# Where layer 2's weights are split into two pieces, and in what order layer 2's own values are

## The chip, the cores and the metric

The kernel runs on one core of a Trainium2 chip, in one launch. The metric is the device time of one execution in microseconds (us); three runs of the kernel before gave 880.49, 882.21 and 882.72, with a median of 882.21. The core's engines are TensorE (PE; its weight loads are PEld), VectorE (DVE), ScalarE (ACT), GpSimd (POOL) and SyncE (SP), whose queue issues the transfers here.

## The reference

```python
attn = softmax(q, -1) @ (softmax(k, 2).T @ v)        # 4 batches, 8 heads, 576 tokens, 64 wide
x = attn as 2304 tokens x 512
x = silu(x @ w_in)  @ w_out                          # 512 -> 2048 -> 512, layer 1
y = mish(x @ w_in2) @ w_out2                         # the same sizes, layer 2; mish(h) = h * tanh(log(1 + e^h))
```

The weights arrive as 64-bit numbers; the kernel puts each together as a 32-bit one.

## The kernel before

**Two pieces.** TensorE multiplies float32 in a rounded form (fp32r). To keep precision each operand is split into a high piece (a cast by ACT) and a low piece (the value minus the high piece, by DVE or POOL), and a product is three matmuls: high by high, high by low, low by high.

**Layer 1** goes over the hidden units in two passes of eight chunks of 128. The second pass takes the tokens in five blocks (`WIDE`: 512, 512, 256, 512, 512). For each block and chunk c there is a first product G1 (x by w_in, 12 matmuls, then Silu on ACT, cast on ACT, subtraction on DVE) and, three chunks later (`SKEW`), a second product G2 (12 matmuls into four banks that collect the output). At the start of a token block the first four G1 stand one after the other. The list `events` holds these blocks; a block is one unit of its plan's time. x lies in the tile `xa`; the split copy `xs` of a token block is made five events before the block begins, and after that this block's part of `xa` is not read again.

**Layer 2's weights** are loaded and put together in that second pass, by a plan with due times (`w_plan`, `plan`): four weight tiles of 128 x 512 (two of w_in2, two of w_out2) for each of eight pairs of chunks. `w_take` asks for the load two takes ahead (three buffers `st`) and does the first step on ACT and DVE, `w_join` the second on DVE. `w_mix` and `o_mix` form sums of them on DVE, since layer 2 forms its products by Strassen and Winograd's scheme with seven products in place of eight. In the kernel before the unsplit sums go to HBM (`q_store`, into `wqf` and `wof`).

**Layer 2** takes the tokens in three strips (s) of 768, and in each the eight pairs of chunks, so 24 pairs, k = 0 to 23. A pair is seven steps. A step is a product (`prod`, six matmuls of 384 columns into bank 6 or 7) and, from k = 2 on, a `half` (nine matmuls of 256 columns) of the second product for the two pairs before. In pairs 0 and 1 three blocks left over from layer 1 stand in three of these places (`l1_rest`). From step 1, 3 and 5 ACT copies bank 6 (`keep`, tile sc); from step 2, 5 and 7 DVE adds bank 7 and the copy (tile hf) and ACT forms Mish; step 6 is Mish alone. `cut` splits a result into a tile g. `sum_g` forms four sums of the last pair's results on POOL, at step 1, and these are split at steps 1 to 4 (`old`). DVE's `gather` adds finished halves to the output in `xb`.

At the change to the next strip seven sums of x are formed (`x2_early` at pairs 6 and 14, `x2_late` at 7 and 15, on POOL) and split into the tiles x (`x2_part`): cast on ACT, and of two parts the first subtracted on DVE, the second on POOL.

In the first strip (k below 8) the weights come back unsplit from `wqf` and `wof` into the buffer `wall`; `q_split` and `o_split` split them there between the other work, on ACT and DVE and on ACT and POOL, and store both pieces in `wq` and `wo`. The halves trail by two pairs, so `o_split` goes on to pair 9. In the other strips the split weights are loaded as they are (1792 KB for w_in2 of one pair, 512 KB for a unit of w_out2; seven units for two pairs).

Every engine carries out its instructions in the order in which the program issues them (class `InOrder`), so an instruction that waits holds up all behind it. In layer 2 this order is that of the lines in `pair`, `fill` and `flush_lows`.

Of the kernel before, what the change touches and what calls it, by code (L numbers as in the profile page):

```python
# [65 lines left out]
def attention_silu_mish(ctx: ExitStack, tc: tile.TileContext, q, k, v, w_in1, w_out1, w_in2, w_out2, out):  # L66
# [25 lines left out]
    Q_PAIR, Q_RING, O_RING, O_NEAR = 3584, 3, 5, 3  # L92
# [33 lines left out]
    wo = [dp.tile([P, 1024], F32, name=f"wo{i}") for i in range(N_UNIT)]  # L126
    wqf = [dp.tile([P, Q_PAIR // 2], F32, name=f"wqf{i}") for i in range(NQ)]
    wof = [dp.tile([P, 512], F32, name=f"wof{i}") for i in range(N_UNIT)]
# [120 lines left out]
    def w_plan(start):  # L249
# [26 lines left out]
        for q in range(NQ):  # L276
            n = 2 * N0 + 4 * q
            a, b, *cs = boxes = [{} for _ in range(4)]
            for i, box in enumerate(boxes):
                plan((when(k + ev * i), w_take, n + i, box), (when(k + ev * i) + 1.0, w_join, box))  # L280
            mix = {}
            h = when(k + ev) + 1.2
            plan((when(k) + 1.4, q_store, a, "t", wqf[q][:, :512]), (h, w_mix, a, b, mix))
            plan((h + 0.4, q_store, b, "t", wqf[q][:, 512:1024]), (h + 0.4, q_store, mix, "t", wqf[q][:, 1024:1536]))
            plan((h + 0.4, q_store, mix, "z", wqf[q][:, 1536:]))
            c0, c1 = cs
            mo = {}
            h = when(k + 3 * ev) + 1.2
            plan((h, o_mix, c0, c1, mo))
            for box, what, half, i in (  # L290
                (c0, "t", 0, 0), (c0, "t", 1, 4), (c1, "t", 0, 1), (c1, "t", 1, 5), (mo, "t", 0, 3), (mo, "t", 1, 2), (mo, "z", 0, 6)
            ):
                plan((h + 0.4, q_store, box, what, wof[q // 2 * 7 + i][:, q % 2 * HD:(q % 2 + 1) * HD], half * HD))
            k += 4 * ev
# [26 lines left out]
    def w_mix(a, b, mix):  # L321

        a, b = (t["t"].bitcast(F32).rearrange("p (l n) -> p l n", l=2) for t in (a, b))
        u, z = (pools["tm"].tile([P, 512], U32, tag="wt", name="wt") for _ in range(2))
        mix["t"], mix["z"] = u, z
        u, z = (t.bitcast(F32).rearrange("p (l n) -> p l n", l=2) for t in (u, z))
# [447 lines left out]
    sums, lows = {}, []  # L774
# [34 lines left out]
    def x2_part(s, m):  # L809
        for k in range(2):  # L810
            t = sums[(s, m, k)]
            S.copy(x2[m][:, k, 0], t)
            lows.append((V if k == 0 else G, x2[m][:, k], t))

    def flush_lows():
        for e, to, t in lows:
            e.tensor_tensor(out=to[:, 1], in0=t, in1=to[:, 0].bitcast(F32), op=ALU.subtract)
        lows.clear()


    def q_unit(k, u):
        at, n = k % Q_RING * Q_PAIR + u * 1024, 256 if u == 3 else 512
        return wall[:, at:at + 2 * n].rearrange("p (i n) -> p i n", i=2)
# [12 lines left out]

    def q_split(k, *units):
        if k < NQ:
            for u in units:
                split(q_unit(k, u), V)  # L840
            if 3 in units:
                SP.dma_start(wq[k], wall[:, k % Q_RING * Q_PAIR:(k % Q_RING + 1) * Q_PAIR].bitcast(F32))
# [348 lines left out]
```

## Time and profile before

| | |
|---|---|
| median of three runs | 882.21 us |
| the profiled execution | 886.13 us, of which its span 884.3 |
| busy: PE, PEld, DVE, ACT, POOL | 841.9, 784.9, 556.1, 439.6, 233.5 us |
| DMA | 170.80 MB, mean 193 GB/s |
| mean granted TensorE clock | 0.985 |

All times in the profile are those of one execution, in us from its first instruction. Layer 1's second pass runs from about 285 to 472 us, layer 2 from there to the end. A row of the timeline gives a start, a length and an instruction; in brackets stand the time that the engine idled before it, and what ended the wait. Since nearly all calls go through one helper, most instructions carry the same line, L59, and are told apart by tiles.

### The profile page before, as it was taken

What the parts mean: (1) busy time and instruction counts of PE and PEld (TensorE: products, weight loads), DVE (VectorE), ACT (ScalarE), POOL (GpSimd) and SP (SyncE); (2) the same over time, 40 slices, a digit from 0 to 9 for tenths busy, and PEclk for the clock granted to TensorE, in tenths of its full rate; (3) what the DMA queues carried; (4) which work ended last, traced back from release to release, by engine and by line L of the source; (5) the groups of instructions that cost most, each with busy time, mean ns of one, the idle gap of its engine ahead of it and who ended that gap; (6) DMA issues with size and microseconds to landing.
All of it is one profiled execution on the core that took longest, in us unless ns stands there. A gap on an engine that the chain in (4) does not pass through costs nothing.

```text
span 884.3 us, 14216 instructions
## 1 busy us (share of the span) xinstructions
PE 841.9 (95%) x5314; PEld 784.9 (89%) x5314; DVE 556.1 (63%) x1043; ACT 439.6 (50%) x870; POOL 233.5 (26%) x239
## 2 busy tenths in 40 slices
PE   7799999999999999999999897978899998999997
PEld 6688988899999888898888887977899998999997
DVE  5898466673276566756753675658566658555555
ACT  5887254563245444444356555646444436444441
POOL 3035111221000000000031554469623438131310
PEclk9899999999999999999999999999899999999999
DMA  9986311310034359847626688889797666686634
GB/s 242 246 207 135 91 36 36 72 37 1 1 119 128 110 174 300 262 160 248 214 90 214 248 303 314 295 291 325 270 329 269 231 245 233 241 302 221 209 135 144
DMA packets 101028, 170.80 MB, mean 193 GB/s; under 512 B 34400, under 2 KB 73312, under 8 KB 97888
## 3 DMA queue, kind: packets, MB, share of 16 engines
q1 hardware_dynamic: 100960, 169.90, 58.6%
q8 instruction: 42, 0.69, 0.3%
q14 instruction: 26, 0.21, 0.1%
HBM read 121.11 MB, written 48.76 MB: 192 GB/s over the span
## 4 chain that ended last, share of the span: by engine, by line
PE 75%; DVE 6%; DMA 6%; ACT 5%; POOL 3%; issue 3%; SPq 2%; POOLq 0%; DVEq 0%; ACTq 0%
PE psum L59 57%; PE psum L57 18%; DMA wall<-wof 3%; DVE g L59 1%; DVE xb L59 1%; SPq L57 1%; POOL x L59 1%; DVE hf L59 1%; DMA xa<-in_k_dram 1%; DMA st<-in_moe_w_in_dram 1%; ACT g L59 1%; ACT xa L57 1%; ACT hf L59 1%; ACT wall L59 1%; POOL hf L59 1%
## 5 line engine op out<-in xcount | busy, mean ns | idle before, releaser
L59 PE MATMUL psum<-x,wall 128*128 128x384 f32 x1008 | 212.6, 348 | 24.8 <-DVE hf L59 17.1
L59 PE MATMUL psum<-wall,g 128*128 128x256 f32 x1512 | 207.2, 284 | 2.5 <-DVE xb L59 2.5
L59 PEld LDWEIGHTS psum<-wall,g 128*128 128x128 f32 x1512 | 202.0, 192 | 3.0 <-DVE xb L59 3.0
L59 PEld LDWEIGHTS psum<-x,wall 128*128 128x128 f32 x1008 | 176.1, 193 | 30.1 <-DVE hf L59 20.2
L59 DVE TENSOR_TENSOR g<-hf,g 128x384 fp32r<-128x384 f32 x168 | 109.7, 671 | 62.5 <-ACT g L59 61.9
L59 POOL TENSOR_TENSOR hf<-hf 128x384 f32<-128x384 f32 x92 | 98.2, 1068 | 143.8 <-ACT hf L59 138.4
L59 PE MATMUL psum<-g,wall 128*128 128x512 f32 (+2 forms) x624 | 129.7, 361 | 0.0
L59 PEld LDWEIGHTS psum<-g,wall 128*128 128x128 f32 x624 | 109.6, 189 | 14.9
L59 PE MATMUL psum<-xs,wall 128*128 128x512 f32 (+2 forms) x588 | 122.4, 362 | 0.0
L59 PEld LDWEIGHTS psum<-xs,wall 128*128 128x128 f32 x588 | 102.7, 188 | 14.9
L59 DVE TENSOR_TENSOR xb<-psum,xb 128x768 f32<-128x768 f32 (+2 forms) x94 | 80.1, 867 | 38.5 <-PE psum L59 38.4
L57 PE MATMUL psum<-xs,wall 128*128 128x384 f32 x468 | 100.4, 355 | 2.8 <-ACT gf L57 1.8
L59 ACT ACTIVATE hf<-hf 128x384 f32<-128x384 f32 x72 | 37.9, 526 | 112.6 <-DVE hf L59 112.6
L59 ACT CAST g<-hf 128x384 fp32r<-128x384 f32 x168 | 82.3, 513 | 21.5 <-POOL hf L59 16.6
L57 PEld LDWEIGHTS psum<-xs,wall 128*128 128x128 f32 x468 | 82.7, 193 | 7.0 <-ACT gf L57 3.2
L57 PE MATMUL psum<-g,wall 128*128 128x384 f32 x432 | 84.8, 343 | 0.0
L59 POOL TENSOR_TENSOR x<-xb,x 128x384 fp32r<-128x384 f32 x16 | 19.6, 1242 | 240.0 <-ACT x L59 240.0
L57 PEld LDWEIGHTS psum<-g,wall 128*128 128x128 f32 x432 | 74.7, 188 | 1.0 <-DVE g L57 0.2
L59 ACT ACTIVATE gf<-psum 128x512 f32<-128x512 f32 (+2 forms) x49 | 26.6, 543 | 95.8 <-PE psum L59 94.8
L59 DVE TENSOR_TENSOR g<-gf,g 128x512 fp32r<-128x512 f32 (+2 forms) x49 | 30.5, 624 | 66.5 <-ACT g L59 66.0
L59 ACT COPY sc<-psum 128x384 f32<-128x384 f32 x72 | 34.3, 477 | 56.8 <-PE psum L59 56.3
L59 POOL TENSOR_TENSOR wall<-wall 128x512 fp32r<-128x512 f32 x28 | 38.4, 1370 | 70.7 <-ACT wall L59 64.3
(133 smaller groups left out, 875.7 us busy)
## 6 DMA issues: line engine op xcount, KB each, us to landing
wall<-wq SPq DMA_DIRECT2D x16, 1792.0 KB, 8.7
wall<-wo SPq DMA_DIRECT2D x56, 512.0 KB, 4.2
st<-in_moe_w_in_dram SPq DMA_DIRECT2D x32, 512.0 KB, 5.0
st<-in_moe_w_out_dram SPq DMA_DIRECT2D x32, 512.0 KB, 4.5
wq<-wall SPq DMA_DIRECT2D x8, 1792.0 KB, 6.8
wo<-wall SPq DMA_DIRECT2D x28, 512.0 KB, 4.4
wof<-wt SPq DMA_DIRECT2D x56, 128.0 KB, 4.2
wall<-wof SPq DMA_DIRECT2D x28, 256.0 KB, 6.1
```

The costliest lines, as they stand in the source:

```text
L57: return call(*args, **kwargs)
L59: self.last = call(*args, **kwargs)
```

## The change

Layer 2's weights are split in layer 1's second pass, before they go to HBM. `t_high` casts a tile on ACT into one of eight strips of 512 columns in `xa` (the first 1024 tokens of x, which the second pass has read by then), `t_low` subtracts on POOL in place, `z_high` and `z_low` do the same for the narrow sums, and `put` stores both pieces into `wq` and `wo`, which are now the only copies. `wqf`, `wof`, `q_split`, `o_split` and their stores in layer 2 go; the first strip loads `wq` and `wo` as the others do. The pool of weight tiles (`tm`) has ten buffers in place of eight.

In layer 2, `cut` and `x2_part` no longer issue their casts and subtractions at once: they put them into the lists `casts` and `lows` with a due time in steps. `background`, once in each step, issues those that are due, and more while the time it counts for ACT and DVE (`COST` each, of `LONG` in a step) has room; `settle` issues what the next product or half needs. `sum_g` moves from step 1 to step 2, and all four sums enter the list there. At the strip changes POOL keeps three subtractions (`X_POOL`) of seven; before layer 2 DVE does all of them. At the end four sums on DVE are followed by their splits through the same list.

```diff
--- before.py
+++ after.py
...
@@ w_plan
-                plan((when(k + ev * i), w_take, n + i, box), (when(k + ev * i) + 1.0, w_join, box))
-            plan((when(k) + 1.4, q_store, a, "t", wqf[q][:, :512]), (h, w_mix, a, b, mix))
...
+                plan((when(k + ev * i), w_take, n + i, box), (when(k + ev * i + 1.0), w_join, box))
+            for i, mix in ((0, w_mix), (2, o_mix)):
+                a, b = boxes[i:i + 2]
+                m, z = {}, {}
+                h = k + ev * (i + 1) + 1.3
+                plan((when(h), mix, a, b, m, z))
+                for j, box in enumerate((a, b, m)):
+                    plan((when(h + 0.7 + 0.2 * j), t_high, box), (when(h + 1.1 + 0.2 * j), t_low, box))
+                plan((when(h + 1.3), z_high, z), (when(h + 1.7), z_low, z))
+                h += 1.9
+                if mix is w_mix:
+                    for j, box in enumerate((a, b, m)):
+                        to = wq[q][:, j * 1024:(j + 1) * 1024]
+                        plan((when(h), put, box, "hi", to[:, :512]), (when(h), put, box, "t", to[:, 512:]))
+                    plan((when(h), put, z, "t", wq[q][:, 3072:]))
...
+    def t_high(box):
+        i = strips["at"] = (strips["at"] + 1) % 8
+        box["hi"] = xaT[:, i % KC, i // KC * 512:(i // KC + 1) * 512]
+        S.copy(box["hi"].bitcast(F32R), box["t"].bitcast(F32))
+    def t_low(box):
+        G.tensor_tensor(out=box["t"].bitcast(F32R), in0=box["t"].bitcast(F32), in1=box["hi"], op=ALU.subtract)
...
+    def put(box, what, to):
+        t = box[what].bitcast(F32)
+        SP.dma_start(to, t if len(to.shape) == 2 else t.rearrange("p (i n) -> p i n", i=2))
...
@@ x2_part
-            S.copy(x2[m][:, k, 0], t)
-            lows.append((V if k == 0 else G, x2[m][:, k], t))
+            t, to = sums[(s, m, k)], x2[m][:, k]
+            if now is None:
+                S.copy(to[:, 0], t)
+                V.tensor_tensor(out=to[:, 1], in0=t, in1=to[:, 0].bitcast(F32), op=ALU.subtract)
+            else:
+                later_cut(to, t, now, due, (m, s), G if k and m in X_POOL else V)
+    X_POOL = (T2, T1, B22)
+    def later_cut(home, t, ready, due, tag, e=None):
+        serial[0] += 1
+        casts.append((due - 1, serial[0], ready, home, t, tag, V if e is None else e))
...
+    def settle(tag, now):
+        for z in [z for z in casts if z[5] == tag]:
+            one_cast(z, now)
+        for z in [z for z in lows if z[5] == tag]:
+            one_low(z)
+    def background(now, a_room, v_room):
+        while casts:
+            z = min((z for z in casts if z[2] <= now), default=None)
+            if z is None or (z[0] > now and a_room < COST):
+                break
+            a_room -= COST
+            one_cast(z, now)
+        while lows:
+            z = min((z for z in lows if z[2] <= now or z[0] <= now), default=None)
+            if z is None or (z[0] > now and v_room < COST):
+                break
+            v_room -= COST if z[6] is V else 0.0
+            one_low(z)
...
     def q_load(k):
-        if k < NQ:
-            for u in range(4):
-                w = q_unit(k, u)[:, 1].bitcast(F32)
-                SP.dma_start(w, wqf[k][:, u * 512:u * 512 + w.shape[1]])
-        elif k < NS * NQ:
+        if k < NS * NQ:
             SP.dma_start(wall[:, k % Q_RING * Q_PAIR:(k % Q_RING + 1) * Q_PAIR].bitcast(F32), wq[k % NQ])
-    def split(w, e):
-        S.copy(w[:, 0], w[:, 1].bitcast(F32))
-        e.tensor_tensor(out=w[:, 1], in0=w[:, 1].bitcast(F32), in1=w[:, 0].bitcast(F32), op=ALU.subtract)
...
-            split(o_slot(m).rearrange("p (i n) -> p i n", i=2), G)
-            SP.dma_start(wo[m], o_slot(m).bitcast(F32))
...
+    COST, SUM_AT = 0.58, 2
+    LONG, SHORT, REST = 2.13, 1.05, 3.77
-    def cut(k, name, t):
+    def cut(k, name, t, ready):
         home = slots.pop(0)
         gp[(k, name)] = home
-        S.copy(home[:, 0, :BLK], t)
-        lows.append((V, home, t))
+        use = (k // 2 * 2 + 2) * 7 + 1 + 2 * [z[0] for z in PHASES].index(name) + k % 2
...
+        later_cut(home, t, ready, use - 1, (k, name))
...
@@ pair
+        for i, (a, m, ps, start) in enumerate(ORDER, 1):
+            now = 7 * k + i
+            settle((m, s), now)
+            prod(k, a, m, ps, start)
+            a_room = v_room = LONG if k > 1 else REST if (k, i) in L1_AT else SHORT
...
+            if i == SUM_AT and k:
+                sum_g(k - 1, G, now)
...
+            background(now, a_room, v_room)
+            if i == 1 and q == NQ - 2 and s + 1 < NS:
+                x2_early(s + 1)
+            if i == 7:
+                q_load(k + Q_RING)
+            if pend:
+                half(*pend.pop(0))
...
-            for nm, nb in (("g", SKEW + 1), ("xs", 1), ("gf", 2), ("st", 3), ("tm", W_WAIT)):
+            for nm, nb in (("g", SKEW + 1), ("xs", 1), ("gf", 2), ("st", 3), ("tm", W_WAIT + 2)):
```

Three places in the engines' orders. On ACT, at the change to the last token block of layer 1 (gf is Silu's result, wt a weight tile, xs the split x of the block), before:

```order
L59 ACTIVATE gf<-psum 128x512
L59 CAST g<-gf 128x512
L59 CAST xs<-xa 128x512 x4
L59 ACTIVATE wt<-st 128x512 x3
L59 ACTIVATE gf<-psum 128x512
```

and there now:

```order
L59 ACTIVATE gf<-psum 128x512
L59 CAST g<-gf 128x512
L59 CAST xa<-wt 128x512 x3
L59 CAST xs<-xa 128x512 x4
L59 CAST wt<-wt 128x256
L59 ACTIVATE wt<-st 128x512 x2
L59 CAST xa<-wt 128x512 x3
L59 CAST wt<-wt 128x256
L59 ACTIVATE wt<-st 128x512
L59 CAST xa<-wt 128x512 x3
L59 ACTIVATE gf<-psum 128x512
```

Nine wide casts and two narrow ones stand now between the last Silu of one token block and the first of the next; each waits for DVE's sums.

On ACT in pair 4 of layer 2, from the copy of step 1 to that of step 5 (wall is the weight buffer), before:

```order
L59 COPY sc<-psum 128x384
L59 CAST g_4774<-hf 128x384
L59 ACTIVATE hf<-hf 128x384
L59 CAST g_4767<-hf 128x384
L59 CAST g_4768<-hf 128x384
L59 CAST wall<-wall 128x512 x2
L59 COPY sc<-psum 128x384
L59 CAST g_4775<-hf 128x384
L59 CAST wall<-wall 128x512
L59 CAST g<-hf 128x384
L59 CAST wall<-wall 128x512
L59 COPY sc<-psum 128x384
```

and there now:

```order
L59 COPY sc<-psum 128x384
L59 ACTIVATE hf<-hf 128x384
L59 CAST g_4848<-hf 128x384
L59 COPY sc<-psum 128x384
L59 CAST g_4842<-hf 128x384
L59 CAST g_4841<-hf 128x384
L59 CAST g_4849<-hf 128x384
L59 CAST g<-hf 128x384
L59 COPY sc<-psum 128x384
```

The weight casts are gone, and the casts of the last pair's four sums stand together behind the copy of step 3.

On POOL at the change from the first strip to the second, between the sums of pair 6 and those of pair 7 (hf), before:

```order
L59 TENSOR_TENSOR hf<-hf 128x384 x4
L59 TENSOR_TENSOR wall<-wall 128x512
L59 TENSOR_TENSOR x_4532<-xb,x_4532 128x384
L59 TENSOR_TENSOR wall<-wall 128x512
L59 TENSOR_TENSOR x_4533<-xb,x_4533 128x384
L59 TENSOR_TENSOR xb<-xt,xb 128x384 x2
L59 TENSOR_TENSOR x_4534<-xt,x_4534 128x384
L59 TENSOR_TENSOR xb<-xb,xt 128x384 x2
L59 TENSOR_TENSOR wall<-wall 128x512
L59 TENSOR_TENSOR x_4535<-xb,x_4535 128x384
L59 TENSOR_TENSOR x_4536<-xb,x_4536 128x384
L59 TENSOR_TENSOR wall<-wall 128x512
```

and there now:

```order
L59 TENSOR_TENSOR hf<-hf 128x384 x8
L59 TENSOR_TENSOR xb<-xt,xb 128x384 x2
L59 TENSOR_TENSOR xb<-xb,xt 128x384 x2
L59 TENSOR_TENSOR x_4626<-xt,x_4626 128x384
L59 TENSOR_TENSOR x_4627<-xb,x_4627 128x384
L59 TENSOR_TENSOR hf<-hf 128x384 x4
```

Two subtractions of x stand now before pair 7's sums; a third comes behind them, and the others are DVE's.

## Rows read from the trace of the kernel before

**Rows 1.** Busy by stretch: length, PE, PEld, DVE, ACT, POOL, clock, DMA share, GB/s
```profile
471.90:500.60 28.70, 25.67 (x122) 22.84 (x121) 16.23 (x27) 17.40 (x35) 9.35 (x8) 0.94 0.75 270
...
500.60:635.00 134.40, 114.45 (x737) 110.83 (x736) 90.37 (x126) 73.98 (x159) 79.94 (x67) 0.95 0.81 290
635.00:739.40 104.40, 104.40 (x737) 104.40 (x736) 65.54 (x96) 49.82 (x107) 43.11 (x40) 1.00 0.74 270
739.40:759.00 19.60, 17.08 (x107) 16.55 (x106) 14.06 (x20) 9.20 (x21) 10.68 (x9) 0.91 0.58 206
759.00:863.40 104.40, 104.40 (x737) 104.40 (x736) 60.76 (x95) 46.60 (x99) 29.84 (x28) 1.00 0.64 224
```
**Rows 2.** Timeline of PE: start, length, instruction, tiles, shape, count
```profile
476.94 3.34 PE L59 MATMUL psum<-x,wall 128*128 128x384 f32 x18
480.12 2.88 PE L59 MATMUL psum<-g,wall 128*128 128x512 f32 x12
482.84 3.33 PE L59 MATMUL psum<-x,wall 128*128 128x384 f32 x18
...
652.06 1.23 PE L59 MATMUL psum<-x,wall 128*128 128x384 f32 x6
...
666.97 1.23 PE L59 MATMUL psum<-x,wall 128*128 128x384 f32 x6
```
**Rows 3.** Timeline of the tail, idle time before in brackets
```profile
869.69 0.50 PE L59 MATMUL psum<-wall,g 128*128 128x256 f32 x2 [1.80 <-DVE xb L59]
```
**Rows 4.** Waits in 500:640: who waited for whom, us, times, longest
```profile
ACT g L59 <- POOL hf L59: 13.4, 6, 6.1
...
PE psum L59 <- DVE hf L59: 12.9, 6, 4.1
PE psum L59 <- ACT sc L59: 5.6, 4, 3.4
```
**Rows 5.** Timeline of pair 4, ACT and PE
```profile
549.48 0.62 ACT L59 CAST wall<-wall 128x512 fp32r<-128x512 f32 x1 [3.42 <-DMA wall<-wof]
...
550.52 1.85 PE L59 MATMUL psum<-x,wall 128*128 128x384 f32 x6 [3.40 <-ACT sc L59]
```
**Rows 6.** Timeline of pair 16, POOL and PE
```profile
740.64 5.27 POOL L59 TENSOR_TENSOR x<-xb,x 128x384 fp32r<-128x384 f32 x4
...
745.87 4.44 POOL L59 TENSOR_TENSOR hf<-hf 128x384 f32<-128x384 f32 x4
...
748.88 1.53 PE L59 MATMUL psum<-x,wall 128*128 128x384 f32 x4 [2.32 <-DVE hf L59]
```
**Rows 7.** Groups of instructions in 500.6:635: count, busy us, mean ns, idle before
```profile
L59 ACT CAST wall<-wall 128x512 fp32r<-128x512 f32 (+1 forms) x46 | 26.1, 589 | 3.4 <-DMA wall<-wof 3.4
...
L59 DVE TENSOR_TENSOR wall<-wall 128x512 fp32r<-128x512 f32 (+1 forms) x22 | 17.7, 804 | 15.7 <-ACT wall L59 15.7
...
L59 POOL TENSOR_TENSOR wall<-wall 128x512 fp32r<-128x512 f32 x24 | 33.0, 1374 | 47.6 <-ACT wall L59 41.2 <-PE psum L59 6.4
```
**Rows 8.** Busy time by stretch, two wide token blocks of layer 1's second pass
```profile
344.00:366.00 22.00, 22.00 (x99) 18.22 (x98) 14.23 (x32) 8.87 (x17) 0.00 (x0) 1.00 0.81 264
...
396.00:438.00 42.00, 42.00 (x187) 34.80 (x186) 27.82 (x57) 18.34 (x31) 0.00 (x0) 1.00 0.76 248
```
**Rows 9.** DMA issues: tiles, count, KB each, median us from issue to landing
```profile
st<-in_moe_w_in_dram SPq DMA_DIRECT2D x32, 512.0 KB, 5.0
```
**Rows 10.** Timelines of POOL and DVE, one beside the other and DVE alone
```profile
600.55 1.61 POOL L59 TENSOR_TENSOR wall<-wall 128x512 fp32r<-128x512 f32 x1
...
606.68 1.37 DVE L59 TENSOR_TENSOR g<-hf,g 128x384 fp32r<-128x384 f32 x1
...
860.51 0.56 DVE L59 TENSOR_TENSOR g<-hf,g 128x384 fp32r<-128x384 f32 x1 [0.19 <-ACT g L59]
```
**Rows 11.** Busy time by stretch of 20 us, two slices with full DMA queues
```profile
60.00:80.00 20.00, 19.75 (x160) 17.73 (x159) 19.04 (x48) 16.80 (x33) 7.63 (x11) 1.00 0.80 149
...
560.00:580.00 20.00, 17.87 (x127) 17.67 (x126) 10.23 (x17) 9.41 (x20) 11.49 (x10) 1.00 0.94 332
```

More of the change, by code (lines that the diff above doesn't have):

```diff
@@ L125, in attention_silu_mish @@
     wq = [dp.tile([P, Q_PAIR], F32, name=f"wq{i}") for i in range(NQ)]
[L126 to L128 removed]
+    wo = [dp.tile([P, 7 * 1024], F32, name=f"wo{i}") for i in range(NQ // 2)]
     lx = ExitStack()
@@ L277, in w_plan @@
             n = 2 * N0 + 4 * q
-            a, b, *cs = boxes = [{} for _ in range(4)]
+            boxes = [{} for _ in range(4)]
             for i, box in enumerate(boxes):
-                plan((when(k + ev * i), w_take, n + i, box), (when(k + ev * i) + 1.0, w_join, box))
-            mix = {}
-            h = when(k + ev) + 1.2
-            plan((when(k) + 1.4, q_store, a, "t", wqf[q][:, :512]), (h, w_mix, a, b, mix))
[L284 to L293, printed above, removed]
+                plan((when(k + ev * i), w_take, n + i, box), (when(k + ev * i + 1.0), w_join, box))
[14 more added lines that the diff above has]
+                else:
+                    to = wo[q // 2].rearrange("p (u f n) -> p u f n", u=7, f=2)[:, :, q % 2]
+                    for box, at_ in ((a, to[:, 0:5:4]), (b, to[:, 1:6:4]), (m, to[:, 2:4])):
+                        plan((when(h), put, box, "hi", at_[:, :, :HD]), (when(h), put, box, "t", at_[:, :, HD:]))
+                    plan((when(h), put, z, "t", to[:, 6]))
             k += 4 * ev
@@ L319, in w_low, with two, mix_tiles, w_mix @@
         V.tensor_tensor(out=w[:, 1], in0=box["t"].bitcast(F32), in1=w[:, 0].bitcast(F32), op=ALU.subtract)
[L321 to L326, printed above, removed]
+    def two(t):
+        return t.bitcast(F32).rearrange("p (l n) -> p l n", l=2)
+    def mix_tiles(m, z):
+        m["t"], z["t"] = (pools["tm"].tile([P, 512], U32, tag="wt", name="wt") for _ in range(2))
+        return two(m["t"]), two(z["t"])
+    def w_mix(a, b, m, z):
+        a, b = two(a["t"]), two(b["t"])
+        u, z = mix_tiles(m, z)
         V.tensor_tensor(out=u[:, 0], in0=b[:, 0], in1=b[:, 1], op=ALU.add)
@@ L773, in attention_silu_mish @@
     x2 = {}
-    sums, lows = {}, []
+    sums = {}
     def x2_tok(s, k):
@@ L807, in x2_late, with x2_part @@
             G.tensor_tensor(out=t, in0=t2 if m == T3 else t, in1=t if m == T3 else t2, op=ALU.subtract)
-    def x2_part(s, m):
+    def x2_part(s, m, now=None, due=0):
         for k in range(2):
-            t = sums[(s, m, k)]
-            S.copy(x2[m][:, k, 0], t)
-            lows.append((V if k == 0 else G, x2[m][:, k], t))
[L815 to L818, printed above, removed]
@@ new lines, in attention_silu_mish, with one_cast, one_low @@
+    casts, lows, serial = [], [], [0]
+    X_POOL = (T2, T1, B22)
+    def later_cut(home, t, ready, due, tag, e=None):
+        serial[0] += 1
+        casts.append((due - 1, serial[0], ready, home, t, tag, V if e is None else e))
+    def one_cast(task, now):
+        due, n, _, home, t, tag, e = task
+        casts.remove(task)
+        S.copy(home[:, 0, :BLK], t)
+        lows.append((due + 1, n, now + 1, home, t, tag, e))
+    def one_low(task):
+        _, _, _, home, t, _, e = task
+        lows.remove(task)
+        e.tensor_tensor(out=home[:, 1], in0=t, in1=home[:, 0].bitcast(F32), op=ALU.subtract)
@@ L1153, in attention_silu_mish @@
     k = NS * NQ - 1
-    sum_g(k, V)
-    for name in ("s2", "s1", "s3", "s4"):
-        cut(k, name, f32s[(k, name)])
-        flush_lows()
+    sum_g(k, V, 7 * k + 7)
     pend.extend((k // 2, i, f) for i in range(7) for f in range(2))
-    while pend:
+    for now in range(7 * k + 8, 7 * k + 22):
+        background(now, 0.6, 0.6)
         half(*pend.pop(0))
```

167 lines of the change are left out of this document (61 added, 106 removed).

## The prediction

> **What bounds the kernel now.** I read the busy times by stretch first, then PE's timeline, then the waits inside the stretches that lose time, then the groups that the change touches. PE is the bound: it is busy 841.9 us of 884.3. Layer 2 from its third pair of chunks (k = 2) cuts into equal pieces of seven pairs, seven, one, seven, and a tail [rows 1]. Pairs 9 to 15 and 17 to 23 take 104.40 us each, PE busy throughout: 14.91 us a pair, which is seven steps of 2.13 us (one product of six matmuls, one half of nine), as the starts of one product and of its seventh successor show [rows 2]. That is the floor. Pairs 2 to 8 do the same work in 134.40 us, so they lose 30.0 us; pair 16 takes 19.60 us and loses 4.7 [rows 1]. Of the 30.0 only 19.95 is idle; in the rest PE ran at the lower of its clock's levels after a wait (granted share 0.95 over the stretch, 1.00 in both floors). Pairs 0 and 1, with three leftover blocks of layer 1 between them, take 28.70 us [rows 1]. Three products take 3.18 us and a block 2.72 [rows 2], so 14 x 1.06 + 3 x 2.72 = 23.0 would do: 5.7 lost. In the tail PE stands 1.8 us before its last ten halves [rows 3]. In all 5.7 + 30.0 + 4.7 + 1.8 = 42.2 us, and nothing is lost in layer 1's second pass, where PE is busy 22.00 of 22.00 and 42.00 of 42.00 us [rows 8].
>
> Why pairs 2 to 8 lose time: there PE's waits end on DVE's sum hf or ACT's copy sc, and ACT's on POOL's sums hf [rows 4]. The 3.4 us wait at 550.5 is the plainest: ACT stood 3.42 us before a cast of a weight whose load had not landed, the copy that PE needs stood behind it in ACT's queue, and PE then ran its six matmuls in 1.85 us instead of 1.23 [rows 5, 2]. Pair 16 has no weight left to split; its wait comes from POOL, where four subtractions of x stand ahead of the four sums [rows 6].
>
> **What goes.** In pairs 2 to 8 ACT's 46 weight casts (26.1 us), DVE's 22 subtractions (17.7) and POOL's 24 (33.0) go [rows 7], with all stores of split weights and the small loads. Of these 76.8 us nothing lay on PE by itself; what they held up did. Without them these pairs have the work and loads of pairs 9 to 15, which lose nothing. So 30.0 less one block change like pair 16's, 25.3, is the first term. The order ahead of pair 6 stays: four x operations before the sums on POOL. In pair 14 the same order cost nothing [rows 1], since no weight waited in POOL's queue before them.
>
> The list is the second term. At the block changes (pairs 8 and 16, 4.7 us each) POOL has three subtractions of x instead of seven, and the rest stand on DVE by need. What is late next: the two pairs of x sums stay on POOL ahead of pair 7's sums, with two subtractions behind them, some 4 x 1.3 + 2 x 1.3 us, in three steps of 2.13. I leave 1 us of loss at each, 2 of 9.4. From both sides: nothing left, or 9.4 as before. Pairs 0 and 1: splits go from all three engines, and DVE takes over four subtractions of x before the pairs, under layer 1's blocks. The chain copy, sum, Mish is then alone on ACT and DVE; I leave 1 of 5.7 (bounds 0 and 5.7). The tail: DVE sums first and then subtracts one tile at a time as its cast comes, so the first late half is ready under the five before it; 1.8 goes, or stays. In the steady pairs sums start one step later and casts follow by due time; I allow 1 us of new waits, between nothing and the second rival's price.
>
> **What comes.** Layer 1's second pass gets 48 casts of 512 and 16 of 256 on ACT, as many subtractions on POOL, and twice the stored bytes. ACT is busy 8.87 of 22.00 and 18.34 of 42.00 us there [rows 8]. A block of twelve matmuls takes 22.00 / 99 x 12 = 2.67 us there; a pair's weights take 6.05 blocks in the plan, 16.1 us, and add eight casts of at most 0.6 us (589 ns in the mean of such casts [rows 7]), 4.8 us: room enough. What stands behind them on ACT is the silu of the next block; PE has two accumulators for these products, and mostly three blocks of 2.67 us lie before it needs the same one again, so ACT may be some 8 us late; but where a token block starts four products follow each other, and it is one block less the silu itself. POOL, idle there, gets 48 x 1.37 [rows 7] and 16 of half that, 77 us. Two resources come near their end.
>
> First, DMA. Per pair 1.84 MB more are stored (half of 1792 + 3.5 x 512 KB) in 16.1 us, 114 GB/s: 264 becomes 378 in 344:366, and 248 becomes 370 in 396:438 (2.8 pairs of stores). Their shares of 0.81 and 0.76 [rows 8] scale to 1.16 and 1.13: the queue would run behind by 3.5 us in the first stretch and 5.5 in the second. A weight load lands in 5.0 us [rows 9] and is asked for two takes, 8.0 us, ahead, so ACT waits some 0.5 and 2.5 us for it. On SP the stores wait for POOL, and the next weight load stands behind them.
>
> Second, DVE beside POOL. With both on SBUF tiles they take turns: DVE's 384-wide subtraction lasts 1.37 us instead of 0.56, POOL's 512-wide one 1.61 [rows 10]. So a POOL subtraction holds back one DVE operation by about 0.8 us; at four in each half pair, DVE's 14.23 of 22.00 us becomes 23.1, its 27.82 of 42.00 becomes 44.5: 1.1 and 2.5 us too much, if DVE has work at every turn.
>
> I take 5 us of PE's waits for both together, at the two wide token blocks that start after such a stretch (the first after 366, the last of the pass at 438). Below: nothing, since 8 us of slack may swallow all. Above: 3.5 + 5.5 + 1.1 + 2.5 = 12.6.
>
> The Trainium skill says in "SBUF — State Buffer", section "SBUF: two separate sides", that the pair of ports which VectorE and GpSimd share is an exclusive lock for a whole instruction, and that the loser blocks fully. By it each of the 64 subtractions takes its full time from DVE, 77 us. The rows only partly agree: four POOL operations beside DVE's took 5.27 us [rows 6], 1.32 each, where DVE's 0.56 and POOL's 1.11 (four in 4.44) add up to 1.67, so part of each overlaps; I go by the rows. The rule's own result is the fifth rival.
>
> The Trainium skill's "DMA: Bandwidth & Descriptors", section "Specifications", gives about 358 GB/s as HBM's limit for one core. By it alone the second stretch would run behind by (370 - 358) / 358 x 42 = 1.4 us, not 5.5; the fullest slice here moved 332 GB/s at a share of 0.94 [rows 11], near that limit, but with other transfers.
>
> **Sum.** Against the profiled execution: span 884.3, about it 1.8 (its time is 886.1). Off: 25.3 + 7.4 + 4.7 + 1.8 = 39.2. On: 5 + 1 = 6. Net 33.2, a span of 851.1. The median shown, 882.2, is 3.9 below the profiled run; taken from it: **849.0 us**.
>
> **Rivals.**
> 1. *Nothing new waits.* Layer 1 swallows its additions and all idle goes: 882.2 - 42.2 = 840.0, with a residue 840 to 844. For it: layer 1's slack, and 208.8 us of layer 2 without a wait. Against: two resources over their end by the working above.
> 2. *The list waits for POOL.* The sums start a step later, and the casts of the first two sums stand right behind the copy of step 3 on ACT. Four sums take 4.44 us [rows 6], two steps. If ACT stands 1 us in each of 22 pairs and PE with it: 849 + 22 = 871. For: ACT's 13.4 us behind POOL [rows 4]. Against: PE's slack behind that copy is a whole half and product.
> 3. *The list cures neither block changes nor pairs 0 and 1*: 849 + 7.4 + 4.7 = 861. For: pair 16's wait is POOL's own queue. Against: four of its seven x operations are moved.
> 4. *The other side: layer 1 becomes bound by its transfers.* Place: the 61 blocks, some 145 us, in which 16.8 MB of weights come in and 29.4 go out. It eats the whole gain when the 46.2 MB need 145 + 38 us, at 252 GB/s; at 186 GB/s, the rate of the slice 60:80 at full share (149 at 0.80 [rows 11]), they need 248 us, and the time is 849 - 5 + 103 = 947, slower. Against: those are far smaller packets, and 332 GB/s were reached.
> 5. *POOL's subtractions stop DVE for their whole time*: DVE would need, in the two stretches, 14.23 + 2.7 x 4 x 1.37 = 29.0 of 22.00 and 27.82 + 5.2 x 4 x 1.37 = 56.3 of 42.00 us, 21 too much: 849 + 16 = 865.
> 6. *The change doesn't do what it says*: pairs 2 to 8 wait for their loads and not for the splits, so that only small waits go: 882 - 9 = 873. Against: pairs 9 to 15 wait for the same loads, 1792 KB at once, and lose nothing.
>
> **How the numbers follow.** Forecast (845 to 857) 0.46; rival 1 0.19; 2 0.09; 3 0.10; 4 0.03; 5 0.10; 6 0.03. The range 841 to 864 leaves out 2, 4, 6, part of 5 and the bottom of 1, under 0.2. A change under 0.3% can't be told from none. Faster 0.95 (all but rival 4 and the ends of 2 and 6), same 0.02, slower 0.03.
>
> **What would show it.** Right: pairs 2 to 8 at 104.4 to 107 us, no ACT or POOL rows on wall in layer 2; pairs 8 and 16 within 2 us of 14.9; PE idle of a few us in 312:472, ended by ACT's gf, its DMA share above 0.85. Wrong: PE idle of over 12 us there (4 or 5), or a wait on ACT's copy in every pair (2).

## The result and the profile after

The changed kernel takes 868.80 us (median of four runs, 868.10 to 870.11) where the kernel before took 882.19 beside it: a ratio of 0.9853, with a 95% interval of 0.9836 to 0.9871. It is faster, by 13.4 us or 1.5%. The forecast was 849.0 with a range of 841 to 864, so the gain was overestimated by 20 us. The profiled execution's span fell by 17.3 us, from 884.3 to 867.0; the profiled execution of before was 3.9 us above its median, that of after equals its own.

Layer 2 came out as forecast. These are busy times by stretch of the changed kernel, cut at pairs 0, 2, 9, 16 and 17; they answer to [rows 1].

```profile
495.03:518.38 23.35, 23.35 (x121) 21.42 (x120) 8.66 (x14) 11.77 (x24) 5.27 (x5) 1.00 0.63 233
518.38:622.80 104.42, 104.40 (x735) 104.07 (x735) 72.87 (x108) 51.98 (x112) 42.85 (x39) 1.00 0.69 245
623.02:727.42 104.40, 104.40 (x738) 104.40 (x736) 67.98 (x102) 49.46 (x106) 40.31 (x37) 1.00 0.74 259
727.42:742.62 15.20, 15.18 (x107) 14.85 (x106) 13.09 (x18) 9.14 (x22) 6.80 (x7) 1.00 0.77 265
```

Pairs 2 to 8 take 104.6 us in place of 134.4 (the next pair's first product is at 623.02), pair 16 takes 15.2 in place of 19.6, pairs 0 and 1 23.35 in place of 28.70. PE is busy throughout at a granted clock of 1.00. In the tail 0.86 us are left of 1.80 [rows 3]:

```profile
852.36 11.05 PE L59 MATMUL psum<-wall,g 128*128 128x256 f32 x90 [0.86 <-DVE xb L59]
```

From layer 2's first product to the end it is 372.0 us, where it was 412.2 (from 472.10): 40.2 gained.

The rest was lost in layer 1's second pass. Here are PE's rows at the token block starts of the changed kernel, idle time before a row in brackets:

```profile
332.32 5.73 PE L59 MATMUL psum<-xs,wall 128*128 128x512 f32 x24 [1.18 <-ACT gf L59]
...
385.29 4.81 PE L59 MATMUL psum<-xs,wall 128*128 128x256 f32 x24 [10.13 <-ACT gf L59]
...
450.76 5.60 PE L59 MATMUL psum<-xs,wall 128*128 128x512 f32 x24
462.64 8.08 PE L59 MATMUL psum<-xs,wall 128*128 128x512 f32 x24 [6.28 <-ACT gf L59]
```

PE stands three times for a Silu (gf), and once, for 0.34 us, for DVE's part of xs. After the wait it runs slower: the same 24 matmuls take 5.60 us ahead of the last wait and 8.08 behind it. The stretches say the same (length, PE, PEld, DVE, ACT, POOL, clock, DMA share, GB/s):

```profile
344.00:366.00 22.00, 22.00 (x99) 18.21 (x97) 18.00 (x27) 11.28 (x21) 11.32 (x10) 1.00 0.97 323
366.00:396.00 30.00, 19.46 (x120) 17.46 (x119) 25.29 (x38) 14.67 (x34) 15.98 (x12) 0.83 0.96 336
396.00:438.00 42.00, 42.00 (x231) 36.71 (x231) 35.72 (x52) 27.67 (x53) 25.73 (x19) 1.00 0.80 273
438.00:472.00 34.00, 27.72 (x113) 22.38 (x112) 29.70 (x43) 16.16 (x31) 18.80 (x14) 0.90 0.81 284
312.00:472.00 160.00, 142.00 (x692) 119.97 (x691) 136.36 (x196) 87.59 (x170) 88.20 (x64) 0.95 0.82 282
```

The first of these answers to the first stretch of [rows 8]. The third does not answer to the second: the wide block that stood at 393.19 now begins at 407.21, 14.0 us later, and 396 to 407 is the narrow block's. The stretch with the same work is 410 to 452. With it stands the stretch of PE's longest wait:

```profile
371.00:385.00 14.00, 3.82 (x25) 2.96 (x23) 13.66 (x23) 5.75 (x12) 6.98 (x7) 0.78 0.93 304
...
410.00:452.00 42.00, 42.00 (x187) 34.79 (x186) 40.59 (x50) 25.82 (x47) 27.72 (x19) 1.00 0.94 323
```

So DVE has hardly a gap at the two long waits of PE: it is busy 13.66 of 14.00 us around the first and 40.59 of 42.00 ahead of the second (an operation that is held up counts as busy for all its time).

As one measure of this pass I take the time from the first product of its second wide token block to layer 2's first product: 326.64 to 472.10 in the kernel before, 145.46 us, and 325.54 to 495.03 after, 169.49. That is 24.0 us lost: 1.8 in that block, 13.3 in the narrow one, none in the next, 8.9 in the last. With 1.1 us won ahead of it, 40.2 - 24.0 + 1.1 = 17.3.

Why the Silu is late is read on ACT. The first row below is the last Silu of the second wide block, the last row the first of the narrow one:

```profile
366.10 0.58 ACT L59 ACTIVATE gf<-psum 128x512 f32<-128x512 f32 x1
...
371.68 0.67 ACT L59 ACTIVATE wt<-st 128x512 f32<-128x512 f32 x1 [1.72 <-DMA st<-in_moe_w_out_dram]
...
374.76 1.14 ACT L59 CAST xa<-wt 128x512 fp32r<-128x512 f32 x2 [1.91 <-DVE wt L59]
...
382.44 0.66 ACT L59 ACTIVATE wt<-st 128x512 f32<-128x512 f32 x1 [5.67 <-DMA st<-in_moe_w_in_dram]
383.01 1.64 ACT L59 CAST xa<-wt 128x512 fp32r<-128x512 f32 x3
384.56 0.40 ACT L59 CAST wt<-wt 128x256 fp32r<-128x256 f32 x1
384.86 0.38 ACT L59 ACTIVATE gf<-psum 128x256 f32<-128x256 f32 x1
```

Silu to Silu takes 18.8 us, 9.3 of them waits for loads and for DVE's sums. In the kernel before the same two are 12.3 us apart, and ACT waits for PE ahead of the second:

```profile
359.48 0.60 ACT L59 ACTIVATE gf<-psum 128x512 f32<-128x512 f32 x1 [3.61 <-PE psum L59]
...
371.79 0.39 ACT L59 ACTIVATE gf<-psum 128x256 f32<-128x256 f32 x1 [1.50 <-PE psum L59]
```

At the last block no load is late between the two Silus: the casts there wait for DVE, the last of them 5.90 us.

```profile
460.43 1.66 ACT L59 CAST xa<-wt 128x512 fp32r<-128x512 f32 x3 [5.90 <-DVE wt L59]
462.00 0.59 ACT L59 ACTIVATE gf<-psum 128x512 f32<-128x512 f32 x1
```

### The profile page after: what moved, and what is told of

The parts are those of the page before. It is cut to its first block, busy times and chain, and to the rows that moved or that the text cites. A ratio compares the mean times of both kernels' runs of the same rounds, so it can differ in the third digit from the quotient of the medians.

```text
span 867.0 us, 14239 instructions
## 1 busy us (share of the span) xinstructions
PE 832.3 (96%) x5314; PEld 777.1 (90%) x5314; DVE 577.2 (67%) x1025; ACT 440.4 (51%) x874; POOL 266.8 (31%) x261
## 5 line engine op out<-in xcount | busy, mean ns | idle before, releaser
L59 PE MATMUL psum<-x,wall 128*128 128x384 f32 x1008 | 205.3, 339 | 0.0
L59 PE MATMUL psum<-wall,g 128*128 128x256 f32 x1512 | 204.1, 281 | 0.9 <-DVE xb L59 0.9
L59 PEld LDWEIGHTS psum<-wall,g 128*128 128x128 f32 x1512 | 198.5, 189 | 1.1 <-DVE xb L59 1.1
L59 PEld LDWEIGHTS psum<-x,wall 128*128 128x128 f32 x1008 | 172.2, 189 | 1.5 <-DVE x L59 0.7
L59 PE MATMUL psum<-xs,wall 128*128 128x512 f32 (+2 forms) x588 | 128.1, 372 | 17.9 <-ACT gf L59 17.6
L59 PEld LDWEIGHTS psum<-g,wall 128*128 128x128 f32 x624 | 108.9, 188 | 15.2 <-DVE g L59 0.5
L59 POOL TENSOR_TENSOR wt<-wt,xa 128x512 fp32r<-128x512 f32 x48 | 71.6, 1518 | 164.0 <-DVE wt L59 114.6
L59 DVE TENSOR_TENSOR g<-hf,g 128x384 fp32r<-128x384 f32 x168 | 101.9, 638 | 18.4 <-ACT g L59 18.4
L59 ACT CAST g<-hf 128x384 fp32r<-128x384 f32 x168 | 79.2, 513 | 5.0 <-DVE hf L59 3.1
L59 DVE TENSOR_TENSOR hf<-psum,sc 128x384 f32<-128x384 f32 x72 | 40.1, 557 | 55.7 <-ACT sc L59 28.2
L59 DVE TENSOR_TENSOR g<-gf,g 128x512 fp32r<-128x512 f32 (+2 forms) x49 | 40.4, 826 | 48.6 <-ACT g L59 48.3
```

Source lines behind the costliest of these rows:

```text
L59: self.last = call(*args, **kwargs)
```

## Experiments

Theory A: POOL's subtractions stretch DVE's operations, so that its sums are late. B: there are too many bytes, and loads land late. C: the next load is asked for too late. D: the plan brings too many takes due between two Silus. "Lost" is the measure above, less 145.46 us, read from the one profiled execution of each kernel; ratios are to the kernel before, run on the same chip. In experiments 5 and 7 the profiled execution was the slowest of four (854.03 and 850.28 us), in 10 the fastest (843.87).

| kernel | median us | ratio, 95% interval | lost us |
|---|---|---|---|
| the change | 868.80 | 0.9853 (0.9836 to 0.9871) | 24.0 |
| 1: POOL subtracts 64 columns | 856.78 | 0.9699 (0.9678 to 0.9720) | 10.7 |
| 2: thin stores | 866.54 | 0.9813 (0.9795 to 0.9831) | 22.2 |
| 3: subtractions on DVE | 862.13 | 0.9761 (0.9738 to 0.9785) | 17.0 |
| 4: four buffers, sums in strips | 889.58 | 1.0069 (1.0043 to 1.0095) | 43.1 |
| 5: 1 and 2 | 849.64 | 0.9620 (0.9587 to 0.9653) | 8.6 |
| 6: plan's clock | 860.76 | 0.9754 (0.9728 to 0.9780) | 18.4 |
| 7: 3 and 6 | 848.50 | 0.9617 (0.9589 to 0.9645) | 5.7 |
| 8: four buffers | 866.15 | 0.9817 (0.9793 to 0.9842) | 21.7 |
| 9: no list in layer 2 | 878.71 | 0.9963 (0.9946 to 0.9980) | 24.5 |
| 10: 3, 6 and 8 | 846.08 | 0.9584 (0.9562 to 0.9606) | 0.6 |
| 11: 6 and 8 | 859.35 | 0.9731 (0.9677 to 0.9785) | 15.7 |
| 12: 3 and 8 | 857.05 | 0.9701 (0.9658 to 0.9744) | 14.1 |

### 1. POOL's subtractions cut to 64 columns

```diff
-G.tensor_tensor(out=box["t"].bitcast(F32R), in0=box["t"].bitcast(F32), in1=box["hi"], ...
+G.tensor_tensor(out=box["t"].bitcast(F32R)[:, :64], in0=box["t"].bitcast(F32)[:, :64], in1=box["hi"][:, :64], ...
...
```

> The changed kernel with POOL's subtractions of the weight tiles cut to their first 64 columns (the low pieces are wrong beyond them); casts, stores and loads are as in the change. Theory A (turns: POOL's subtractions stretch DVE's operations, DVE's joins come late, and with them the next weight load, ACT's take of it and the Silu behind it): PE's 17.9 us of waits in layer 1's second pass and the low clock behind them go, 846 to 852 us, and DVE's g 512 falls from 826 ns in the mean to about 620. Theory B (bytes: the transfers are too many, loads land late): waits as before, 866 to 870. Theory C (order on SP: the next load is asked for only when one of three buffers is free and stands behind seven stores that wait for POOL): part of it, since POOL is done sooner, 855 to 862.

The loss fell by 13.3 of 24.0 us, the waits at 332 and 462 to 0 and 0.4, though not the one at the narrow block, as PE's timeline of this kernel shows:

```profile
380.42 5.49 PE L59 MATMUL psum<-xs,wall 128*128 128x256 f32 x24 [7.17 <-ACT gf L59]
```

So POOL's work stands behind more than half of the loss. The time, 856.78, lies in C's range and not in A's, and the edit by itself can't part them, since with POOL done sooner the stores and loads behind it on SP are sooner too (the order on SP was not changed by itself in any run). That DVE is held up is seen directly: its g 512 fell to 0.69 us in the mean, from 1.10 in 312:472. The two traces show the stretching where the last block begins. DVE in the changed kernel (a join, the next take's single operation, four additions out of PSUM, a join):

```profile
453.24 1.60 DVE L59 SCALAR_TENSOR_TENSOR wt<-wt,st 128x512 uint32<-128x512 uint32 x1
454.77 1.51 DVE L59 TENSOR_SCALAR st<-st 128x512 uint32<-128x512 uint32 x1
456.20 2.47 DVE L59 TENSOR_TENSOR xb<-psum,xb 128x512 f32<-128x512 f32 x4
458.60 0.67 DVE L59 SCALAR_TENSOR_TENSOR wt<-wt,st 128x512 uint32<-128x512 uint32 x1
```

The same four on DVE in this experiment:

```profile
445.22 0.69 DVE L59 SCALAR_TENSOR_TENSOR wt<-wt,st 128x512 uint32<-128x512 uint32 x1
445.83 0.55 DVE L59 TENSOR_SCALAR st<-st 128x512 uint32<-128x512 uint32 x1
446.30 2.47 DVE L59 TENSOR_TENSOR xb<-psum,xb 128x512 f32<-128x512 f32 x4
448.69 0.68 DVE L59 SCALAR_TENSOR_TENSOR wt<-wt,st 128x512 uint32<-128x512 uint32 x1
```

And POOL in the changed kernel, beside the first three of its rows:

```profile
452.94 4.46 POOL L59 TENSOR_TENSOR wt<-wt,xa 128x512 fp32r<-128x512 f32 x3 [4.06 <-DMA wo<-xa]
457.37 0.72 POOL L59 TENSOR_TENSOR wt<-wt 128x256 fp32r<-128x256 f32 x1
```

### 2. Thin stores

```diff
+        if thin:
+            to, t = (x[:, :64] if len(x.shape) == 2 else x[:, :, :32] for x in (to, t))
...
-plan((when(h), put, z, "t", wq[q][:, 3072:]))
+plan((when(h), put, z, "t", wq[q][:, 3072:], q > 1))
...
-... wq[k % NQ])
+... wq[k % 2])
...
```

> The changed kernel with the stores of pairs 2 to 7 cut to 64 of their columns; layer 2 loads the pieces of pairs 0 and 1 for all (its numbers are wrong, its loads as large as before). The number of transfers, their order and what they wait for stay. Theory B (bytes): DMA share in layer 1's second pass falls to about 0.55, PE's waits there go, 846 to 852 us. Theory A (turns): 864 to 869, DVE's operations as long as now. Theory C (order on SP): 862 to 869, since stores still wait for POOL and loads stand behind them.

The DMA share from 366 to 396 fell from 0.96 to 0.50, yet PE's wait at the narrow block fell only from 10.13 to 8.97 us, and the one at the last block hardly (6.28 to 6.26):

```profile
382.14 5.49 PE L59 MATMUL psum<-xs,wall 128*128 128x256 f32 x24 [8.97 <-ACT gf L59]
...
460.45 7.05 PE L59 MATMUL psum<-xs,wall 128*128 128x512 f32 x24 [6.26 <-ACT gf L59]
```

Bytes are not the cause by themselves; the stores of pairs 0 and 1 were still whole until about 366.

### 3. The subtractions on DVE

```diff
-G.tensor_tensor(out=box["t"].bitcast(F32R), ...
+V.tensor_tensor(out=box["t"].bitcast(F32R), ...
...
-G.tensor_tensor(out=z[:, 1].bitcast(F32R), ...
+V.tensor_tensor(out=z[:, 1].bitcast(F32R), ...
```

> The changed kernel with all subtractions of the weight tiles on DVE in place of POOL: nothing is left out. DVE gets 48 x 0.69 + 16 x 0.42 = 40 us more work, but nobody to take turns with. Theory A (turns): the time that DVE loses beside POOL goes, some 30 to 35 us against 40 added, so PE's waits shrink or stay: 855 to 868. Theory B (bytes): 866 to 870. If DVE's own load decides: 872 to 885.

As A expected, within its range: 7 us less lost. DVE, which now does 64 subtractions more, is busy less than in the changed kernel, 130.40 of 160 us against 136.36, as the pass's row of busy times has it (columns as above):

```profile
312.00:472.00 160.00, 147.12 (x722) 125.42 (x722) 130.40 (x267) 91.81 (x178) 0.00 (x0) 0.96 0.85 293
```

### 4. Four load buffers, the sums' tiles in the strips

```diff
-        while state["dma"] < min(n + 3, len(need)):
+        while state["dma"] < min(n + (4 if n >= 2 * N0 else 3), len(need)):
...
-        m["t"], z["t"] = (pools["tm"].tile(...) for _ in range(2))
+        m["t"], z["t"] = (strip() for _ in range(2))
...
-... ("st", 3), ("tm", W_WAIT + 2) ...
+... ("st", 4), ("tm", W_WAIT) ...
```

> The changed kernel with four load buffers in place of three, and each weight load of layer 2 asked for three takes ahead in place of two; to make room the two tiles of each sum lie in the dead strips of x and the pool of weight tiles has 8 buffers in place of 10. Nothing is left out. Theory C (a load asked for too late): ACT's waits for DMA in layer 1's second pass (27.6 us now) fall under 5, PE's waits go for the most part, 846 to 855 us. Theory A (turns): DVE stays as late, ACT waits on DVE's joins and sums in place of the load, 860 to 868. Theory B (bytes): the queue is as full, 860 to 869.

A miss that says nothing on C: five tiles for each half pair now turn in the eight strips of `t_high`, where three did, and the casts wait for the strips' stores. So its waits in 300:475 say (who waited for whom, us, times, longest):

```profile
ACT xa L59 <- DMA wo<-xa: 26.6, 5, 8.5
...
ACT xa L59 <- DMA wq<-xa: 15.0, 5, 4.6
```

### 5. Both cuts

Edits 1 and 2 together.

> Both cuts at once in the changed kernel: POOL subtracts 64 columns only, and the stores of pairs 2 to 7 carry 64 columns (layer 2 uses the pieces of pairs 0 and 1 for all; the numbers are wrong). By itself the first left a wait of 7.2 us at the start of the narrow token block, the second 9.0 us there. Theory A+B (each of the two, late DVE and late loads, is enough for that wait): with both gone it goes, 844 to 848 us. Theory D (the order on ACT: the plan counts the entries for a block's start and end as blocks of PE's time, so four takes come due in some 11 us there, and no load can be that fast): 3 us or more stay, 850 to 856.

The median, 849.64, lies between the two ranges, and the four runs spread over both (847.19 to 854.03); the sign that D named is there: 5.0 us of wait are left at the narrow block, with POOL's work and the bytes all but gone. PE's timeline of this kernel:

```profile
377.82 5.49 PE L59 MATMUL psum<-xs,wall 128*128 128x256 f32 x24 [4.97 <-ACT gf L59]
```

### 6. The plan's clock

```diff
-            time.append(time[-1] + (1.0 if blocks[e[1]][e[2]][1] == 512 else Q_SHORT))
+            time.append(time[-1] + (0.0 if e[0] in "XE" else 1.0 if blocks[e[1]][e[2]][1] == 512 else Q_SHORT))
...
-    Q_END, Q_SHORT = 2.0, 0.3
+    Q_END, Q_SHORT = 2.0, 0.5
```

> The changed kernel, whole, with one change to the plan's clock: the entries for a token block's start and end count nothing (1 each now), and a narrow block counts 0.5 of a wide one (0.3 now), so that takes are spread by PE's own time; one take in place of two or three then stands between two Silus where the narrow block starts. Theory D (the bunching turns late loads into a wait of PE): the 10.1 us at 385 and the low clock behind it go for the most part, 852 to 859 us. Theory A+B (DVE and loads are late everywhere, and the wait only moves): 863 to 870.

Between the two theories: the wait at the narrow block fell from 10.1 to 2.2 us, with 1.5 ahead of it, but 5.4 stay at the last block, and 1.1 came at the block between.

```profile
376.47 4.32 PE L59 MATMUL psum<-xs,wall 128*128 128x256 f32 x24 [2.21 <-ACT gf L59]
...
455.71 7.69 PE L59 MATMUL psum<-xs,wall 128*128 128x512 f32 x24 [5.43 <-ACT gf L59]
```

### 7. The plan's clock and the subtractions on DVE

Edits 3 and 6 together.

> The same plan's clock and, with it, all subtractions of the weight tiles on DVE in place of POOL; nothing is left out. Subtractions on DVE alone gave 0.9761 of the kernel before. If the waits at the two block starts have these two causes: 845 to 852 us. If the bunching plays no part: 858 to 863. If DVE, at 130 of 160 us, now decides: 855 to 865 with waits on its sums.

In the first range: 1.5 and 1.8 us of waits are left, both behind takes that wait for loads.

### 8. Four buffers again

```diff
-... ("st", 3), ("tm", W_WAIT + 2) ...
+... ("st", 4), ("tm", W_WAIT + 1) ...
```

with the load request of experiment 4.

> Four load buffers once more, with each weight load of layer 2 asked for three takes ahead; this time the sums stay in the pool of weight tiles, which has 9 buffers in place of 10, and the strips of x keep their distance. Theory C (the load is asked for too late): ACT's waits for DMA in layer 1's second pass fall from 27.6 us to under 10 and PE's waits with them, 850 to 858. Theory A (DVE beside POOL is late): 862 to 868, the waits turning into waits on DVE.

Theory A's answer: waits for loads became waits for DVE, 33.1 us where the changed kernel has 22.9, and PE hardly gained (8.97 at the narrow block). By itself the early request is worth some 2.3 us, which its interval hardly parts from none (0.9793 to 0.9842, the change 0.9836 to 0.9871). From this kernel's waits in 300:475:

```profile
ACT xa L59 <- DVE wt L59: 33.1, 14, 5.9
```

### 9. No list

```diff
-    X_POOL = (T2, T1, B22)
+    X_POOL = range(7)
...
-    COST, SUM_AT = 0.58, 2
+    COST, SUM_AT = 0.0, 1
...
-        for n, t, d in (("s1", a22, 1), ("s2", a11, 1), ("s3", a21, 2), ("s4", a12, 2)):
+        for n, t, d in (("s1", a22, 0), ("s2", a11, 1), ("s3", a21, 2), ("s4", a12, 3)):
...
-            a_room = v_room = LONG if k > 1 else ...
+            a_room = v_room = 99.0
+            for z in [z for z in lows if z[2] <= now]:
+                one_low(z)
```

> The changed kernel with layer 2's list made powerless: each cast is issued in the step in which its value is there and each subtraction one step later, the four sums stand at step 1 with their casts at steps 1 to 4, and POOL keeps all seven subtractions of x, as in the kernel before; the splits stay in layer 1. Nothing is left out. By the prediction's terms the list is worth 7.4 us at the block changes, 4.7 in pairs 0 and 1 and 1.8 in the tail: 868.8 + 13.9 = 883 us, with pairs 2 to 7 still at 14.9 us and pairs 8 and 16 at some 19.6. The rival: without layer 2's splits the old order has room enough, pairs 8 and 16 within 1 us of 14.9: 869 to 873.

The list is worth 9.9 us. Pairs 2 to 6 keep to 14.9 us without it; pairs 7 and 8 lose 5.1, pairs 15 and 16 3.5, pair 1 2.2. The worst wait is the block change's, on PE's timeline:

```profile
617.88 1.33 PE L59 MATMUL psum<-x,wall 128*128 128x384 f32 x6 [1.78 <-DVE hf L59]
```

The expectation counted 1.8 us for the tail, whose order this edit left as in the change; without it 881 stood against 879 measured.

### 10 to 12. Three edits together, and less one each

> The three changes that left the work whole, together: the plan's clock that counts no time for a block's start and end, the subtractions of the weight tiles on DVE, and four load buffers with 9 weight tiles and loads asked for three takes ahead. Without the buffers it was 848.5 us (0.9617 of the kernel before), with 3.3 us of PE's waits left behind ACT's takes that wait for loads. If the late request is what is left: those waits go, 844 to 847 us. If it is the transfers' rate (share 0.99 to 1.04 in 344:438): no change, 847 to 850.

> The last version less one of its three edits: the plan's clock and the four buffers stay, the subtractions are POOL's again; nothing is left out. Layer 1's second pass from its second wide block on lost 24.0 us in the change, 18.4 with the plan's clock alone, 21.7 with the buffers alone and 0.6 with all three. If POOL beside DVE is a cause that the other two don't cover: 13 us or more are lost, 858 to 864 us. If the late loads and the bunching were all: under 5 us, 847 to 852.

> The last version less the plan's clock: subtractions on DVE and four buffers, takes spread as in the change; nothing is left out. Subtractions on DVE alone left 17.0 us lost. If the bunching at the start of the narrow block is a cause of its own: a wait of 4 us or more stays there, 853 to 860 us. If the load asked for earlier covers it: under 3 us lost, 846 to 849.

With all three, layer 1's pass is whole again, and the kernel takes 846.08 us, 4.2% less than before and faster than the change by 2.7% (0.9584 against 0.9853). Experiment 10's busy times of the pass:

```profile
312.00:472.00 160.00, 159.68 (x798) 136.32 (x797) 133.85 (x276) 98.30 (x191) 0.00 (x0) 1.00 0.87 308
```

With the subtractions back on POOL 15.7 us are lost, without the plan's clock 14.1, without the buffers 5.7, where 0.6 are with all. The first two are clear in the times as well (859.35 and 857.05 against 846.08). The buffers are not: experiment 7, without them, took 848.50, and its interval (0.9589 to 0.9645) overlaps that of 10 (0.9562 to 0.9606); the traces show 3.3 us of waits left without them and 0.3 with them. Taken singly the edits give back 7.0, 5.6 and 2.3 us, 14.9 in all; together 23.4. By the ratios it is 20.0 against 23.7 us, which the intervals don't part, so that the whole is more than its parts is not shown by the times. All three runs came in the range of the theory that names a cause of its own for the edit. In experiment 11 the last block keeps its wait of 6.3 us:

```profile
375.89 4.54 PE L59 MATMUL psum<-xs,wall 128*128 128x256 f32 x24 [3.71 <-ACT gf L59]
...
453.59 7.62 PE L59 MATMUL psum<-xs,wall 128*128 128x512 f32 x24 [6.32 <-ACT gf L59]
```

In 12 the narrow block keeps 5.0 us of wait, as D has it, and the last block the 3.6 us of experiment 3:

```profile
377.03 5.49 PE L59 MATMUL psum<-xs,wall 128*128 128x256 f32 x24 [4.98 <-ACT gf L59]
...
452.46 8.16 PE L59 MATMUL psum<-xs,wall 128*128 128x512 f32 x24 [3.62 <-ACT gf L59]
```

## Why the prediction was wrong

**The step that failed** is the term "5 us of PE's waits for both together" in layer 1's second pass, with its bound of 12.6. It measured 24.0 us: 17.9 of idle time and 6.1 in which PE mostly ran at a lower granted clock (0.83 in 366:396, 0.90 in 438:472; of its two levels, 2.4 and 1.2 GHz, it ran part of the time at the lower). The term counted waits only, though in layer 2 the prediction had read 30.0 us lost with 19.95 idle; for the low clock behind the waits it put nothing. With 24.0 in place of 5 the sum gives 868.0 where 868.8 was measured, but in part by offsets: layer 2 gained 2.0 us more than forecast and 1.1 came ahead of the pass, while the sum took a gain worked out on the profiled execution of before, 3.9 us slower than its median, off the median. The places were near: one wait behind the first stretch, at the narrow block rather than a wide one, one at the last block.

Its working priced each resource by what it lacks over a stretch. For the transfers no such lack shows: their share was 0.97 and 0.94 where 1.16 and 1.13 were forecast, thin stores gave back 1.8 us, and experiment 10 moved 308 GB/s over the pass with nearly no wait, where the change moved 282. For DVE it was half right. In the first stretch DVE was busy 18.00 us where 23.1 of 22.00 were forecast. In the second (410 to 452 now) it was busy 40.59 where 44.5 of 42.00 were, and between 406.61 and 460.73 it idled only 0.5 us: there it did run out, and the last block's wait is for its sums. What the working left out is the chain in program order: take (ACT), join and sums (DVE), casts (ACT), next take, Silu (ACT). Each link waits for the other engine's last one. Beside POOL's bursts the DVE links double, and two such rounds stand between two Silus where the plan counts a block's start and end as time that PE doesn't spend. So PE waited 10.13 us at the narrow block, although DVE had 23.6 us to spare over the whole pass, and with POOL's work and most bytes gone 5.0 us were still left there (experiment 5). The prediction saw that four products follow each other there and that ACT's room is a block less, but spread the half pairs evenly and set "8 us of slack" against the queue's lag. Experiments 11 and 12 show that POOL's work and the plan's bunching were each late enough to be felt by itself (15.7 and 14.1 us lost); for the late load that rests on the waits in the traces alone. The prediction's own sign for this had been PE idle of over 12 us there, and it was 17.9.

**The other terms.**
- Pairs 2 to 8 without the splits: forecast 25.3 us, with 3.7 more for the list. Measured 29.8 together; experiment 9 has 24.9 for the splits (30.0 less its 5.1).
- The list at the block changes: forecast 7.4, measured 8.6 in experiment 9 (5.1 + 3.5). Pairs 8 and 16 came within 0.3 us of 14.9.
- Pairs 0 and 1: forecast 4.7 for the list, measured 5.3, of which only 2.2 is the list's; the rest came with the splits' going.
- The tail: forecast 1.8, measured 0.9; the last halves still wait for DVE's addition (xb).
- The 1 us of new waits in layer 2 did not come.
- A POOL subtraction holds back one DVE operation by about 0.8 us: measured, joins 1.20 us in the mean where 0.69 in experiment 3, single operations 0.84 where 0.42; with g and xs some 43 us for 64 subtractions, 0.7 each. This size was right; its use as a sum over a stretch, without the chain, was not. POOL's subtractions themselves took 88.8 us (1.52 each for the wide, 1.08 for the narrow) where 77 were forecast.

**The rivals.** Rival 2's time, 871, is the nearest, by luck: no pair waits on the copy. Rival 5's, 865, is near too, and its way shows in part: DVE did run out ahead of the last block, but a subtraction cost it 0.7 us and not its full 1.4, and the waits at the narrow block had other causes beside. By the Trainium skill's rule in "SBUF — State Buffer", section "SBUF: two separate sides", POOL would take its full time from DVE; 43 of POOL's 88.8 us of subtractions agree with that only in part. Rival 4's transfers reached 336 GB/s in 366:396, and thin stores changed little.

## What to carry to other kernels

Work moved under a busy engine is to be priced along the chain that stands ahead of the next instruction that PE needs, link by link in program order, and not only by how full each engine is. Look at the places where that instruction has least room: here the starts of token blocks, where a plan's clock and PE's time part. Read each engine's busy share just ahead of that instruction, on the stretch with the same work, and not over the whole pass: DVE had 15% to spare over the pass and next to none at the two long waits. Where several links of a chain are late, an edit of one can turn one wait into another (experiment 8), so take edits out one at a time from the version that works, too, and not only add them one at a time.

## What the runs showed of the hardware

- Work given to POOL beside DVE was not free for DVE: 64 subtractions cost it some 43 us in stretched operations, and 38.5 when it did them itself (31.8 for the 48 wide ones and 16 of some 0.42 in experiment 3).
- Operations with one tile in are held too: the single shift took 1.51 us beside POOL and 0.55 in experiment 1. The four additions out of PSUM were not, 2.47 us beside POOL from 456.20 as without it. The Trainium skill's "SBUF — State Buffer", section "SBUF: two separate sides", names the operations that compete for the shared ports by two SBUF inputs or a two-port mode, which fits the additions. The shift has one tile in and would need such a mode; no run here shows whether it has it.
- The transfers ran at 367 GB/s over 42 us in experiment 7, as the last column of its busy times says:

```profile
396.00:438.00 42.00, 42.00 (x194) 35.08 (x193) 39.02 (x83) 29.07 (x54) 0.00 (x0) 1.00 1.04 367
```

The Trainium skill's "DMA: Bandwidth & Descriptors", section "Specifications", has about 358 for one core; the measurement is above it, and the second stretch's forecast of 370 was within reach.
